# Splitting the last weight quarter four steps later, and issuing the conversion's first loads four steps earlier

## The chip, the cores and the metric

The kernel runs on one core of a Trainium2 chip. A core has five engines that work side by side, each with a queue of its own that it works off in order: PE (matmuls), DVE (vector work), ACT (activations and casts), POOL (GpSimd, here elementwise subtractions and indirect transfers) and SP, which issues most of the DMA transfers. They wait for each other on semaphores. The metric is the device time of one launch in microseconds (us).

## The reference, cut to what matters

Three networks follow each other on 3072 tokens of 320 numbers.

```python
x = attn(r, k, v, w, a, b)                   # a recurrence over 768 positions, 32 heads of 40
# mixture of 8 experts, one expert per token
h = relu(einsum('ecd,edf->ecf', disp, w1))   # 8 x (448 rows here) x 320 -> 1024
y = einsum('ecf,efd->ecd', h, w2)            # -> 320, times the gate's probability
# second network, all tokens; w_in and w_out are float64
h = x @ w_in                                 # 3072 x 320 -> 2048
g = where(h > 0, h, exp(min(h, 0)) - 1)
out = (g @ w_out).astype(float32)            # -> 3072 x 320
```

The change touches only the second and third of them (the experts and the second network).

## The kernel before, in words

The recurrence takes roughly the first 440 us and is not touched. After it, `ffn` runs 14 blocks: blocks 0 to 7 are the experts (448 token rows each, 8 steps), blocks 8 to 13 are the second network (512 rows each, 16 steps). A step (b, f) is one chunk of 128 hidden units of block b. `run` writes the program step by step, and every engine keeps that order. In a step the PE does `s1` (eight matmuls at line 968, which fill a `ph` bank), and then `s2` of an older step: three steps back within the experts, four within the second network. `s2` multiplies the activated chunk into the accumulators `po`. The activation of an expert's chunk is ACT's H (L1097) and DVE's L (L1098). In the second network it is DVE N, ACT E and M, DVE M and E, ACT H, and then L (L1112) on DVE for the first five steps of each sixteen, on POOL for the others.

Precision is kept by splitting every weight into a rounded part and a rest. `Weights.split` does this for a quarter of a weight set in four pieces: one ACT cast of 704 columns (L775) and four POOL subtractions (L780) a piece. The raw quarters lie in two buffers and the split ones in four (`ring`). The last of 20 quarters, number 19, is the fourth quarter of the second network, first read in step (8, 12). Its split goes into the buffer that the second half of expert 7 used, whose last reader is `s2` of step (7, 7). The lag puts that `s2` into step (8, 3). Directly behind it come the evictions of expert 7's accumulators (ACT L1044 and L1046, DVE L1045 and L1047), and these free the banks that the first `s2` of block 8 (L992 to L994) writes.

`extra(b, f)` is called at the end of each step and places the pieces. `more(b, f)` is called from it and moves the conversion on: `Convert.pieces` turns the float64 weights of the second network into float32 by integer work on DVE. Jobs 7 to 27 of 28 are left for this part, 21 of them: nine of 512 columns and twelve of 320. A job is three calls:

- stage 1: SP issues the load of the job after next (L822, L825), DVE does L858 and L859, SP issues the store of the job before (L830, L834);
- stage 2: DVE L864 and L865;
- stage 3: DVE L867, L869, L870.

A first call of its own, ahead of all jobs, issues the loads of the first two jobs. Odd steps make two calls and even steps one, from step (0, 5) on; stage 1 waits for its load. Loads go into three buffers S. SP's queue also carries the fetches of the raw quarters (L801, L803), one at every fourth step, and the tokens of the next block (L1084). A block's tokens are transposed by the PE (`pt`), cast by ACT (L952) and completed by DVE (XL and XS, L953) during the block before it.

Of the kernel before, what the change touches and what calls it, by code (L numbers as in the profile page):

```python
# [742 lines left out]
class Ring:  # L743
# [8 lines left out]
    def next(s, split):  # L752
        k = s.turn[split]
        s.turn[split] += 1
        return s.tile((1, 4, 6, 8)[k % 4], F32R) if split else s.tile((0, 3)[k % 2], F32)
# [39 lines left out]
def expert(nc, ring, w1, w2, e, paired=True):  # L795
    def load(g, R):
        q = R.rearrange("p (f x) -> p f x", x=704)
        c = slice(512 * g, 512 * g + 512)
        for k, (o, r, m) in enumerate(((0, 0, 128), (0, 128, 128), (0, 256, 64), (64, 256, 64))):
            k = min(k, 2)  # L800
            nc.sync.dma_start(out=q[o:o + m, :, 128 * k:128 * k + 128],  # L801
                              in_=w1[e, r:r + m, c].rearrange("p (f x) -> p f x", x=128))
        nc.sync.dma_start(out=q[:, :, 384:704], in_=w2[e, c, :].rearrange("(f p) d -> p f d", p=128))  # L803
    return Weights(nc, ring, load, 8, paired)
# [73 lines left out]
def ahead(W):  # L878

    W.fetch(0)  # L880
    yield
    yield from W.split(0)
    W.fetch(1)


def ffn(tc, nc, cst, disp, xt, w1, w2, w32, out, ring, W0, cv):
# [192 lines left out]
    def rows(src, gate=True):  # L1079

        def load(s, now):
            s.X = s.XF[:, 0:4 * RW].rearrange("p (i d) -> p i d", i=4)
            for i in range(4) if now else (slice(0, 4),):
                nc.sync.dma_start(out=s.X[0:112, i], in_=src[:, i])  # L1084
            yield
            if not gate:
                return
            yield
            g = yield from soft(s)
            for i in range(4):  # L1090
                nc.scalar.mul(s.X[0:112, i, 0:D], s.X[0:112, i, 0:D], g[:, i:i + 1])
            yield
        return load
# [61 lines left out]
    def run(blocks, extra):  # L1155

        n = len(blocks)
        lag, now = [], iter(())
        for b, B in enumerate(blocks):
            nf = B.W.nf  # L1160
            for f in range(nf):
                if f == 0 and b + 1 < n:
                    first, side = blocks[b + 1].load(), blocks[b + 1].prep()
                x = B.s1(f)
                lag.append((B, f, x))
                while len(lag) > B.back:
                    p = lag.pop(0)
                    p[0].s2(*p[1:])
                a, now = now, B.act(*x)
                next(now)  # L1170
                next(a, None)
                if b + 1 < n and next(first, 1) and f >= nf - 6:
                    next(side, None)
                extra(b, f)
        next(now, None)
        if isinstance(B, Turned):
            for p in lag:
                p[0].s2(*p[1:])
        else:
            B.finish([p[1:] for p in lag])  # L1180
# [8 lines left out]
    def experts(r, dyn=False, more=None):  # L1189
        Ws = [W0 if not dyn and e == 0 else expert(nc, ring, w1, w2, e, not dyn) for e in range(8)]  # L1190
        hs = [(W, h) for W in Ws for h in range(2)] + ([] if dyn else [(W2, g) for g in range(4)])

        bl = []
        for e in range(8):
            if dyn:
                src = dv[e, bass.ds(r, 1)].rearrange("r p i d -> (r p) i d")
                dst = yr[SL * e:SL * e + SL, :].rearrange("(i p) d -> p i d", p=112)

                def store(Y, i, dst=dst):
                    if i == 3:  # L1200
                        nc.sync.dma_start(out=dst, in_=Y[0:112])
                bl.append(Block(Ws[e], rows(src), relu, store, P=112))
            else:
                def store(Y, e=e):
                    c = bass.ds(over["base"][e - 1], SL) if e else slice(0, SL)
                    nc.sync.dma_start(out=xt[0:256, c].rearrange("(k p) n -> p k n", p=128), in_=Y[:, 0:2])
                    nc.sync.dma_start(out=xt[256:D, c], in_=Y[0:64, 2])
                    nc.sync.dma_start(out=xt[D:D + 1, c], in_=Y[64:65, 2])
                bl.append(Turned(Ws[e], rows(dv[e, 1], e > 0), relu, store, P=112))
        if dyn:  # L1210
            for _ in ahead(Ws[0]):
                pass
        n = len(hs)

        def fetch(j):
            if j < n:
                hs[j][0].fetch(hs[j][1])

        def split(j):
            if j < n:  # L1220
                yield from hs[j][0].split(hs[j][1])

        def go(x, k):
            for _ in range(k):
                next(x, None)
        go(split(1), 5)
        bl[0].start(0 if dyn else 26)
        fetch(2)
        gen = [iter(())]
        first = iter(()) if dyn else late_gate(bl[0])  # L1230
        next(first, None)

        def extra(b, f):
            if b >= 8:
                next(final, None)
                return
            if b == 0 and f > 1:
                next(first, None)
            i, ph = divmod(8 * b + f, 4)

            late = {(14, 0): 16, (14, 2): 17, (15, 2): 18}.get((i, ph)) if i > 13 else i + 2 if ph == 0 else None
            if late:
                gen[0] = split(late)
                fetch(late + 1)
            go(gen[0], 1 if i < 14 else 2)
            if more:
                more(b, f)
        final = split(19)
        if not dyn:
            bl += [sorted_block(g) for g in range(6)]  # L1250
        run(bl, extra)

    def late_gate(B):

        g = yield from soft(B, "late")
        yield
        p = ps.tile([128, 512], F32, tag="ph", name="pgate")
        for i in range(4):
            nc.tensor.matmul(p[:, 112 * i:112 * i + 112], g[:, i:i + 1].to_broadcast([112, 128]), ident[0:112, 0:112], start=True, stop=True)
        yield  # L1260
        B.G = ap.tile([128, SL], F32, tag="gate", name="gate", bufs=1)
        nc.scalar.copy(B.G, p[:, 0:SL])
# [3 lines left out]
    def sorted_block(g):  # L1266

        def load(s, now):
            s.X = s.XF.rearrange("p (k n) -> p k n", k=3)
            c = slice(512 * g, 512 * g + 512)  # L1270
            nc.sync.dma_start(out=s.X[:, 0:2], in_=xt[0:256, c].rearrange("(k p) n -> p k n", p=128))
            nc.sync.dma_start(out=s.X[0:64, 2], in_=xt[256:D, c])
            f = ap.tile([128, 4], F32, tag="idf", name="idf", bufs=3)
            with nc.allow_non_contiguous_dma("a token's number a row"):
                nc.sync.dma_start(out=f, in_=xt[D:D + 1, c].rearrange("o (i p) -> p (o i)", p=128))
            yield
            yield
            s.id = ap.tile([128, 4], I32, tag="id", name="id", bufs=3)
            nc.vector.tensor_copy(s.id, f)
            yield  # L1280
        def store(Y, i):
            x = nc.gpsimd.indirect_dma_start(  # L1282
                out=out, out_offset=bass.IndirectOffsetOnAxis(ap=B.id[:, i:i + 1], axis=0),
                in_=Y[:, i], in_offset=None, bounds_check=NTOK - 1, oob_is_err=False).ins
            for y in sent:
                tc.declare_no_dep(x, y, reason="scatters write different rows")
            sent.append(x)
            nc.gpsimd.memset(gap, 0.0)
        B = Sorted(W2, load, elu, store, back=4)
        return B  # L1290
# [116 lines left out]
    def more(b, f):  # L1407
        if b == 0 and 0 < f < 5 or b == 1 and f in (2, 7):
            next(ct, None)
        if b or f > 4:  # L1410
            for _ in range(1 + f % 2):
                next(rest, None)
    one = over["one"] = ap.tile([128, 8], F32, name="one", bufs=1)
    nc.gpsimd.memset(one, 1.0)
# [6 lines left out]
    nc.gpsimd.memset(cst["turn"], 0.0)  # L1421
    ct = counts()
    experts(0, more=more)
    for _ in rest:
        pass
# [62 lines left out]
```

## Time and profile before

| | us |
|---|---|
| median of 3 runs | 1066.04 (1063.58 to 1072.04) |
| profiled execution, its own time | 1064.33 |
| its span, first to last instruction | 1062.6 |
| PE busy | 965.8 (91% of the span) |
| DVE busy | 727.8 (68%) |
| POOL busy | 606.5 (57%) |
| ACT busy | 516.9 (49%) |

The mean granted clock of TensorE was 0.941 of full speed. The busy shares are means over stages that differ, so the table says which engine to look at first and not what holds it up. The profile's views used below are the list of waits (who waited for whom), the timeline (one engine's instructions in order, with the idle time before each in brackets and what ended it), the windows (busy time of each engine in a stretch, then PEclk, the share of the DMA engines and GB/s), the groups of instructions by form, and the chain that ended last.

### The profile page before, as it was taken

To read this page: it belongs to the slowest core of one execution; us is meant where nothing else is said; L and a number is where in the kernel's file an instruction comes from. 1 tells how busy PE (TensorE), PEld (TensorE's weight loads), DVE (VectorE), ACT (ScalarE), POOL (GpSimd) and SP (SyncE) were. 2 spreads that over 40 slices of the span, in tenths; PEclk is the share of its full clock that TensorE was granted. 3 is DMA by queue.
4 is the path that set the end of the run, shared out by engine and by line. 5 is a ranking of instruction groups with operands and counts; after the bars stand their busy time and mean duration, and the time that the engine had idled before them with its cause. 6 is when DMAs were issued, how large, how long until landed. Compare 5 with 4: busy or idle time off the path is not lost.

```text
span 1062.6 us, 25351 instructions
## 1 busy us (share of the span) xinstructions
PE 965.8 (91%) x9995; PEld 871.9 (82%) x9995; DVE 727.8 (68%) x1287; ACT 516.9 (49%) x1011; POOL 606.5 (57%) x926
## 2 busy tenths in 40 slices
PE   5869978899899999888999999989999999999993
PEld 4758877798788889677889888869989989989983
DVE  8856756788674677549798963656766767776751
ACT  4646544556463334244535545454555455554551
POOL 4757839899898813456677876733323333323332
PEclk9866988899899889999999999989999999999997
DMA  6768675667654864576877765400101010100000
GB/s 165 163 179 197 168 137 105 151 131 141 139 110 103 192 164 103 155 203 168 230 218 209 221 193 188 161 23 3 48 1 32 19 26 25 26 25 1 26 1 28
DMA packets 180984, 121.67 MB, mean 115 GB/s; under 512 B 105792, under 2 KB 166872, under 8 KB 179224
## 3 DMA queue, kind: packets, MB, share of 16 engines
q1 hardware_dynamic: 176788, 102.89, 39.6%
q0 software_dynamic: 3168, 11.14, 3.0%
q10 hardware_dynamic: 900, 5.93, 2.2%
q8 instruction: 81, 1.33, 0.6%
q14 instruction: 47, 0.39, 0.1%
HBM read 86.87 MB, written 33.05 MB: 113 GB/s over the span
## 4 chain that ended last, share of the span: by engine, by line
PE 28%; issue 10%; POOL 6%; DVE 6%; DMA 4%; ACT 2%; SPq 1%; POOLq 0%; DVEq 0%; ACTq 0%
PE ph L968 14%; PE po L992 4%; PE po L994 4%; PE po L993 4%; POOL ring L780 3%; POOL L L1112 2%; DMA ring<-in_w_dram 2%; DVE L L1098 1%; ACT ring L775 1%; SPq L801 1%; DMA S<-in_w_in_dram 1%; DMA w<-E 1%; POOL out_dram L1282 1%; DVE E L859 1%; DVE M L867 1%
## 5 line engine op out<-in xcount | busy, mean ns | idle before, releaser
L780 POOL TENSOR_TENSOR ring<-ring,ring 128x64 fp32r<-128x64 f32 (+2 forms) x320 | 195.7, 647 | 90.0 <-ACT ring L775 87.7
L1112 POOL TENSOR_TENSOR L<-E,H 128x512 fp32r<-128x512 f32 x66 | 87.6, 1327 | 185.8 <-ACT H L1111 148.2
L968 PE MATMUL ph<-XH,ring 128*128 128x512 f32 (+1 forms) x640 | 172.9, 392 | 4.4 <-DVE L L1098 3.9
L968 PEld LDWEIGHTS ph<-XH,ring 128*128 128x128 f32 x640 | 117.4, 193 | 19.6 <-DVE L L1098 4.5
L1105 ACT ACTIVATE E<-N 128x512 f32<-128x512 f32 x96 | 60.7, 633 | 143.7 <-DVE N L1104 88.0
L992 PE MATMUL po<-ring,H 128*128 128x320 f32 x384 | 119.6, 311 | 5.5 <-ACT Y L1044 5.3
L353 POOL TENSOR_TENSOR X<-X,ring 128x60 f32<-128x60 f32 (+19 forms) x170 | 114.9, 676 | 13.3
L994 PE MATMUL po<-ring,L 128*128 128x320 f32 x384 | 119.6, 311 | 1.5 <-POOL L L1112 1.5
L993 PE MATMUL po<-ring,H 128*128 128x320 f32 x384 | 119.4, 311 | 0.0
L1104 DVE TENSOR_SCALAR N<-ph 128x512 f32<-128x512 f32 x96 | 65.9, 686 | 47.4 <-PE ph L968 47.0
L968 PE MATMUL ph<-XL,ring 128*128 128x512 f32 (+1 forms) x320 | 97.6, 386 | 0.0
L968 PE MATMUL ph<-XS,ring 128*128 128x512 f32 (+1 forms) x320 | 97.5, 386 | 0.0
L351 POOL TENSOR_TENSOR ring<-X,ring 128x60 f32<-128x60 f32 (+19 forms) x108 | 74.2, 687 | 39.0 <-DMA ring<-dab 18.2
L992 PEld LDWEIGHTS po<-ring,H 128*128 128x128 f32 x384 | 72.6, 189 | 10.5 <-ACT Y L1044 5.7
L993 PEld LDWEIGHTS po<-ring,H 128*128 128x128 f32 x384 | 72.7, 189 | 4.1
L994 PEld LDWEIGHTS po<-ring,L 128*128 128x128 f32 x384 | 72.9, 190 | 2.0 <-POOL L L1112 2.0
L1109 DVE SCALAR_TENSOR_TENSOR M<-E,M 128x512 f32<-128x512 f32 x96 | 70.7, 736 | 5.5 <-ACT M L1106 5.5
L775 ACT CAST ring<-ring 128x704 fp32r<-128x704 f32 x80 | 61.4, 779 | 21.3 <-issue 8.2
L1110 DVE SCALAR_TENSOR_TENSOR E<-ph,M 128x512 f32<-128x512 f32 x96 | 66.4, 691 | 7.8
L968 PEld LDWEIGHTS ph<-XL,ring 128*128 128x128 f32 x320 | 61.1, 191 | 10.8
L968 PEld LDWEIGHTS ph<-XS,ring 128*128 128x128 f32 x320 | 60.8, 190 | 10.8
L1111 ACT CAST H<-E 128x512 fp32r<-128x512 f32 x96 | 59.2, 617 | 15.1 <-DVE E L1110 12.0
(238 smaller groups left out, 2164.2 us busy)
## 6 DMA issues: line engine op xcount, KB each, us to landing
ring<-in_w_dram SPq DMA_DIRECT2D x16, 640.0 KB
ring<-in_w_dram SPq DMA_DIRECT2D x32, 256.0 KB
RVU<-in_d_in_dram SPq DMA_DIRECT2D x48, 160.0 KB
dab<-AB SPq DMA_DIRECT2D x24, 256.0 KB
ring<-in_e_in_dram ACTq DMA_DIRECT2D x18, 321.6 KB
ring<-w SPq DMA_DIRECT2D x4, 1408.0 KB
disp<-ring SPq DMA_DIRECT2D x8, 575.8 KB
ring<-in_w_dram SPq DMA_DIRECT2D x32, 128.0 KB
```

Source lines behind the costliest of these rows:

```text
L351: nc.gpsimd.tensor_tensor(tv, X[:, 0:n, s:s + 1].to_broadcast([128, n, m]), N[:, s:s + 1, s + 1:e].to_broadcast([128, n, m]), op=ALU.mult)
L353: nc.gpsimd.tensor_tensor(X[:, 0:n, s + 1:e], X[:, 0:n, s + 1:e], tv, op=ALU.subtract)
L775: s.nc.scalar.copy(B[:, 0:704], r)
L780: s.nc.gpsimd.tensor_tensor(B[:, to], r[:, q], B[:, q].bitcast(F32), op=ALU.subtract)
L968: nc.tensor.matmul(p, l, r[:, 0:s.T], start=i == 0, stop=i == len(seq) - 1)
L992: nc.tensor.matmul(o, H[:, c], hb, start=f == 0, stop=False)
L993: nc.tensor.matmul(o, H[:, c], lb, start=False, stop=False)
L994: nc.tensor.matmul(o, L[:, c], hb, start=False, stop=f == s.W.nf - 1)
L1104: nc.vector.tensor_scalar(N, p, 0.0, None, op0=ALU.min)
L1109: nc.vector.scalar_tensor_tensor(out=M, in0=E, scalar=1.0, in1=M, op0=ALU.add, op1=ALU.mult)
L1110: nc.vector.scalar_tensor_tensor(out=E, in0=p, scalar=0.0, in1=M, op0=ALU.max, op1=ALU.add)
L1112: eng.tensor_tensor(L, E, H.bitcast(F32), op=ALU.subtract)
```

## The change

In block 8, quarter 19 is split in steps 4 to 7 and no longer in steps 0 to 3. In step (0, 1) the conversion makes its first call, which only issues loads. All later calls keep their steps, so each does the stage that followed before.

```diff
         def extra(b, f):
             if b >= 8:
-                next(final, None)
+                if b > 8 or f > 3:
+                    next(final, None)
                 return
...
     def more(b, f):
         if b == 0 and 0 < f < 5 or b == 1 and f in (2, 7):
             next(ct, None)
-        if b or f > 4:
-            for _ in range(1 + f % 2):
+        if b or f > 4 or f == 1:
+            for _ in range(1 if f == 1 and not b else 1 + f % 2):
                 next(rest, None)
```

The first place is ACT's queue at the start of block 8. Before:

```order
L1097 ACTIVATE H<-ph 128x448
L775 CAST ring_9053<-ring_8985 128x704
L1105 ACTIVATE E<-N 128x512
L1106 ACTIVATE M<-N 128x512
L1111 CAST H<-E 128x512
L775 CAST ring_9053<-ring_8985 128x704
L1105 ACTIVATE E<-N 128x512
L1106 ACTIVATE M<-N 128x512
L1111 CAST H<-E 128x512
L775 CAST ring_9053<-ring_8985 128x704
L1044 COPY Y<-po 128x448
L1046 COPY half<-po 64x448
```

And now, in the same place:

```order
L1097 ACTIVATE H<-ph 128x448
L1105 ACTIVATE E<-N 128x512
L1106 ACTIVATE M<-N 128x512
L1111 CAST H<-E 128x512
L1105 ACTIVATE E<-N 128x512
L1106 ACTIVATE M<-N 128x512
L1111 CAST H<-E 128x512
L1044 COPY Y<-po 128x448
L1046 COPY half<-po 64x448
```

The three casts of the split stood ahead of the eviction of expert 7; now all four stand behind it, and so do POOL's subtractions. PE's rows are the same in both.

The second place is SP's queue in expert 0, from the tokens of block 1 on (`ring` rows are fetches of raw quarters). Before:

```order
L1084 DMA X<-disp 112x4x329
L801 DMA ring_6517<-in_w_dram 128x4x128 x2
L801 DMA ring_6517<-in_w_dram 64x4x128 x2
L803 DMA ring_6517<-in_w_dram 128x4x320
L801 DMA ring_6667<-in_w_dram 128x4x128 x2
L801 DMA ring_6667<-in_w_dram 64x4x128 x2
L803 DMA ring_6667<-in_w_dram 128x4x320
L822 DMA S_6715<-in_w_in_dram 128x1024
L822 DMA S_6717<-in_w_in_dram 128x1024
L822 DMA S_6719<-in_w_in_dram 64x1024 x2
```

And now:

```order
L1084 DMA X<-disp 112x4x329
L801 DMA ring_6517<-in_w_dram 128x4x128 x2
L801 DMA ring_6517<-in_w_dram 64x4x128 x2
L803 DMA ring_6517<-in_w_dram 128x4x320
L822 DMA S_6554<-in_w_in_dram 128x1024
L822 DMA S_6556<-in_w_in_dram 128x1024
L801 DMA ring_6671<-in_w_dram 128x4x128 x2
L801 DMA ring_6671<-in_w_dram 64x4x128 x2
L803 DMA ring_6671<-in_w_dram 128x4x320
L822 DMA S_6719<-in_w_in_dram 64x1024 x2
```

Two loads of 512 KB each have moved ahead of one fetch of a raw quarter; the third load has kept its place behind it.

The third place is DVE's queue from the end of step (0, 5) on. Before:

```order
L953 TENSOR_TENSOR XL<-pt,XH 128x448
L858 TENSOR_SCALAR N<-S_6715 128x512
L859 SCALAR_TENSOR_TENSOR E<-S_6715,N 128x512
L1098 SCALAR_TENSOR_TENSOR L<-ph,H 128x448
L953 TENSOR_TENSOR XS<-pt,XS 64x448
L864 TENSOR_SCALAR N<-E 128x512
L865 SCALAR_TENSOR_TENSOR M<-S_6715,N 128x512
L1098 SCALAR_TENSOR_TENSOR L<-ph,H 128x448
L867 TENSOR_TENSOR M<-M,E 128x512
L869 TENSOR_SCALAR N<-S_6715 128x512
L870 SCALAR_TENSOR_TENSOR E<-N,M 128x512
L858 TENSOR_SCALAR N<-S_6717 128x512
```

And now:

```order
L953 TENSOR_TENSOR XL<-pt,XH 128x448
L858 TENSOR_SCALAR N<-S_6554 128x512
L859 SCALAR_TENSOR_TENSOR E<-S_6554,N 128x512
L864 TENSOR_SCALAR N<-E 128x512
L865 SCALAR_TENSOR_TENSOR M<-S_6554,N 128x512
L1098 SCALAR_TENSOR_TENSOR L<-ph,H 128x448
L953 TENSOR_TENSOR XS<-pt,XS 64x448
L867 TENSOR_TENSOR M<-M,E 128x512
L869 TENSOR_SCALAR N<-S_6554 128x512
L870 SCALAR_TENSOR_TENSOR E<-N,M 128x512
L1098 SCALAR_TENSOR_TENSOR L<-ph,H 128x448
L858 TENSOR_SCALAR N<-S_6556 128x512
```

An odd step did stage 3 of one job and stage 1 of the next, and an even step stage 2. Now an odd step does stages 1 and 2 of a job and the even step behind it stage 3.

## Rows read from the trace of the kernel before

**Rows 1.** Chain that ended last, second network: start, us, what.

```profile
712.02 1.86 PE ph L968 x8
...
943.99 1.87 PE ph L968 x8
```

**Rows 2.** Waits of PE, 446 to 712 us: total, times, longest.

```profile
PE po L992 <- ACT Y L1044: 5.3, 1, 5.3
PE ph L968 <- DVE L L1098: 3.9, 2, 3.4
...
PE po L1032 <- DVE Y L1045: 2.1, 2, 1.8
```

**Rows 3.** Timeline, PE and ACT, block 8: start, us, engine, [idle before <- releaser].

```profile
696.30 0.36 PE L1041 MATMUL po<-H,ring 128*128 128x448 f32 x1
696.75 0.78 ACT L775 CAST ring<-ring 128x704 fp32r<-128x704 f32 x1 [8.23 <-issue]
703.25 0.52 ACT L1044 COPY Y<-po 128x448 f32<-128x448 f32 x1
703.83 0.64 PE L992 MATMUL po<-ring,H 128*128 128x320 f32 x1 [5.30 <-ACT Y L1044]
...
710.10 0.31 PE L992 MATMUL po<-ring,H 128*128 128x320 f32 x1
```

**Rows 4.** Windows: busy PE, PEld, DVE, ACT, POOL; then PEclk, DMA share, GB/s.

```profile
703.00:706.00 3.00, 2.17 (x8) 2.17 (x9) 2.63 (x6) 1.64 (x4) 2.11 (x4) 0.50 0.33 123
```

**Rows 5.** Costliest groups of the page: busy, mean ns, idle before, releaser.

```profile
L1112 POOL TENSOR_TENSOR L<-E,H 128x512 fp32r<-128x512 f32 x66 | 87.6, 1327 | 185.8 <-ACT H L1111 148.2
```

**Rows 6.** Timeline, SP, DVE and PE, expert 0.

```profile
455.89 0.60 SPq L803 DMA_DIRECT2D ring<-in_w_dram  x1
...
468.92 2.54 SPq L822 DMA_DIRECT2D S<-in_w_in_dram  x4
...
477.44 0.43 DVE L858 TENSOR_SCALAR N<-S 128x512 int32<-128x512 int32 x1 [7.41 <-DMA S<-in_w_in_dram]
...
479.19 1.08 PE L968 MATMUL ph<-XH,ring 128*128 128x448 f32 x4 [3.44 <-DVE L L1098]
```

**Rows 7.** Timeline, PE, at three seams between experts.

```profile
493.46 0.44 PE L1031 MATMUL po<-H,ring 128*128 128x448 f32 x1 [2.61 <-DVE Y L1050]
...
500.24 0.74 PE L933 MATMUL pt<-ident,X 112*128 112x112 f32 x4
...
552.21 0.37 PE L1031 MATMUL po<-H,ring 128*128 128x448 f32 x1
...
560.71 0.55 PE L933 MATMUL pt<-ident,X 112*128 112x112 f32 x4
...
604.22 0.37 PE L1031 MATMUL po<-H,ring 128*128 128x448 f32 x1
...
609.11 0.97 PE L968 MATMUL ph<-XH,ring 128*128 128x448 f32 x4
```

**Rows 8.** Groups by form, DVE, 469 to 632 us: busy, mean ns.

```profile
L867 DVE TENSOR_TENSOR M<-M,E 128x512 f32<-128x512 f32 x9 | 8.3, 922 | 0.0
L869 DVE TENSOR_SCALAR N<-S 128x512 int32<-128x512 int32 x9 | 6.9, 768 | 0.0
L865 DVE SCALAR_TENSOR_TENSOR M<-S,N 128x512 f32<-128x512 uint32 x9 | 6.9, 766 | 0.3
L870 DVE SCALAR_TENSOR_TENSOR E<-N,M 128x512 f32<-128x512 int32 x9 | 6.9, 766 | 0.3
L864 DVE TENSOR_SCALAR N<-E 128x512 int32<-128x512 int32 x9 | 4.0, 448 | 0.1
```

**Rows 9.** Windows, columns as in Rows 4.

```profile
464.00:466.00 2.00, 1.55 (x10) 1.28 (x9) 1.55 (x3) 1.70 (x4) 1.97 (x4) 1.00 0.00 0
```

**Rows 10.** Timeline, POOL and DVE, expert 7.

```profile
663.73 12.57 POOL L780 TENSOR_TENSOR ring<-ring,ring 128x176 fp32r<-128x176 f32 x24
667.41 8.92 DVE L1279 CAST id<-idf 128x4 int32<-128x4 f32 x1
```

## The prediction

> **What bounds the kernel now.** I read the chain that ended last first, because only what lies on it can shorten the run. From 712.02 to 943.99 us it is the PE and nothing else: 65 rows of eight matmuls, 231.97 / 64 = 3.62 us apart [rows 1]. A step of the second network takes 3.62 us, and what the PE gains before block 8 moves the rest forward as it is. So the question is where the PE stood still before that. PE's own list of waits for 446 to 712 us answers it [rows 2]: one wait of 5.3 us for an ACT eviction, one of 3.4 us for DVE's L, two of 2.1 us together for a DVE eviction. A fourth, of 2.61 us, is in rows 7. The change touches the causes of all four.
>
> The timeline of block 8 shows the first [rows 3]. The last matmul that reads the old split buffer ends at 696.30 + 0.36 = 696.66. Only then, at 696.75, ACT starts the cast of quarter 19's first piece, after 8.23 us idle. Behind that cast, in ACT's queue, stand two more casts and the activations of steps (8, 1) and (8, 2), and behind these the eviction L1044, which starts at 703.25. The PE restarts at 703.83 after 5.30 us idle. Then it is slow: the window from 703 to 706 us has a granted clock of 0.50, the 1.2 GHz level [rows 4]. From 703.83 to 710.10 it needs 6.27 us for one step.
>
> The timeline of expert 0 shows the second [rows 6]. SP issues the first four S loads at 468.92, and DVE has stood idle 7.41 us, since 470.03, when it starts stage 1 at 477.44. L of the step stands behind it, and the PE loses 3.44 us.
>
> **The change part by part, and the sum.**
>
> *The split in steps 4 to 7.* The four casts leave their place ahead of the eviction, so L1044 can start when its bank is complete, before 696.66. From the start of L1044 to the PE's restart took 0.58 us [rows 3]. The PE has `s1` of its own until 698.53 (703.83 less 5.30), 1.87 us after 696.66, so I leave nothing of the wait. The slow step goes with it, since the PE ran without a pause up to there. Gain: 5.30 + (6.27 - 3.62) = 7.95 us. Ends: 5.3 if the clock falls all the same, 7.95 if not; I take the upper one.
>
> *The same work, later.* Four casts of 0.78 us [rows 3] and sixteen subtractions of 12.57 / 24 = 0.52 us [rows 10] come into steps 4 to 7. POOL's piece of 2.1 us and its own L of 1.33 us [rows 5] are 3.4 us of a step of 3.62 in steps 6 and 7; in 4 and 5 POOL has no L. What hides them is the lag of four steps, 14.5 us between L and the matmul that needs it. Without that cover, POOL's 2.1 us for each of two steps is 4.2 us. Quarter 19 is read in step 12 and is ready four steps earlier. Cost taken: 0.
>
> *The early loads.* SP issues two loads at 456.49 (455.89 + 0.60) [rows 6], some 0.6 us each (2.54 / 4). The next fetch in SP's queue belongs to a step three steps on, so it is not held. In the trace 1.5 MB landed from 468.92 to 477.44, behind a fetch, which is 5.7 us for these 1.0 MB. From 464 to 466 us the DMA engines moved nothing [rows 9], so the earlier fetch is over by 464, and the loads are there by 469.7 at the latest; stage 1 asks at 470.03. Gain: 3.44 us of the PE; at the other end, if they come with the fetch as now, 0.
>
> *The regrouped stages.* Stage 3 of a wide job costs 0.922 + 0.768 + 0.766 = 2.46 us, stage 2 costs 0.448 + 0.766 = 1.21 us [rows 8]. In the odd step ahead of each eviction DVE had stages 3 and 1; now it has 1 and 2, so 1.24 us less stands ahead of L1045 and L1050. Nothing is added: the 21 jobs do the same seven instructions each.
>
> *The seams between experts.* In a full-speed stretch the PE does `s2`, `s1`, `s2` in 609.11 - 604.22 = 4.89 us [rows 7]. At the first seam it waits 2.61 us and then needs 500.24 - 493.46 = 6.78 us for these, so 2.61 + 1.89 = 4.50 us are lost. At the third, 560.71 - 552.21 = 8.50 us hold the same work and the wait: 3.61 us lost. The rest of the DVE-eviction waits is 2.1 - 1.8 = 0.3 us [rows 2]. At the first seam DVE comes out 7.41 - 3.44 = 3.97 us earlier against the PE, and 1.24 for the regrouping, which is more than the 2.61 it was late: all 4.50 go. At the third only the 1.24 is sure against 1.8 late; I leave 0.55 and no slow step.
>
> Sum: 7.95 + 3.44 + 4.50 + 3.61 + 0.3 - 0.55 = 19.25 us. The profiled execution took 1064.33, so 1045.1. It lies 1.7 us below the median of the runs shown, so the median comes to 1046.8; I say **1047**.
>
> **A rule against it.** DVE's cast of 128x4 numbers took 8.92 us and ended at 676.33, while POOL ran 24 subtractions that ended at 676.30 [rows 10]. So one form of DVE instruction waits until POOL pauses. Stage 1 and stage 2 hold such single-input forms, and the change puts them back to back. Against a large cost: L869 and L864 are the same instruction on the same shape, and the dearer of them takes 0.768 us against 0.448 [rows 8], so the price of a neighbour on POOL was 0.3 us there and not a burst. The Trainium skill ("GPSIMD Engine Reference", section 1, Specifications) says that GpSimd shares its SBUF interfaces with VectorE, with contention for VectorE instructions in a two-port mode or with two SBUF inputs. By that rule the conversion could lose what the regrouping gives, and the sum would be the 11.4 us of the first rival below; the 8.92 us agree with it, the 0.768 us only faintly.
>
> **Rivals.**
> - *DVE stays late in the experts.* A wide job takes 2.46 + 1.21 us of it in two steps of 4.89 / 3 x 4 = 6.5 us, before stage 1, two L and the transposed tokens are counted, so removing one idle stretch may only shift the lateness to another seam. For it: the third seam was late with no load wait before it. Against: 1.24 us less ahead of every eviction. Then 7.95 + 3.44 = 11.4 remain: 1054.6. Late loads belong here too.
> - *The last seam's wait moves on.* The pieces in steps 4 to 7 hold POOL's L and DVE's catching up, and the PE stops once for 4.2 us and does one slow step of 2.65. For it: 3.4 of 3.62 us. Against: a lag of 14.5 us. Gain 19.25 - 6.85 = 12.4: 1053.6.
> - *Slower.* The back-to-back stages run into POOL's pieces as the 8.92 us cast did, and DVE becomes the bound of the experts. If each of 21 conversions loses 1 us on the path, half a piece, the time is 1066.0 - 7.95 + 21 = 1079. It decides at 7.95 / 21 = 0.38 us each, with the other gains of the experts gone. L869's 0.3 us speaks against it, and so does that POOL's bursts there are pieces and not 24 in a row.
> - *It does not do what it says.* The loads move but the eviction is still late because DVE's half of it (L1045) is: nothing but 3.4 us, 1062.6.
>
> **How the numbers follow.** Forecast 0.64; DVE stays late 0.16; wait moves on 0.10; no effect at the seams 0.04; slower 0.06. A measurement of this kernel can tell about 1% from no change, 10.7 us: faster is below 1055.4. The forecast and half of the first two rivals, which lie at that line, give 0.64 + 0.08 + 0.06 = 0.78; the rest of them and the case without effect give 0.16; slower 0.06. Below, the range ends where the 0.55 us go too and the median's offset is absent, with 2 us for its scatter: 1042. Above, it takes in both middle rivals, with 2 us for the same: 1057. That leaves out the last two, 0.10, and the tails of the others.
>
> **What would show it.** In the changed profile: ACT L1044 at block 8 starts within 1 us of its matmuls' end, and PE has no wait for it and PEclk stays at 1.00 there; DVE's L858 shows no idle for S in expert 0, and S is issued some 12 us earlier; no PE wait over 0.6 us for L1045 or L1050; L858, L864 and L869 keep their means within 0.2 us. I am wrong if DVE's busy time in the experts grows by more than a few us, if a PE wait for L (L1112) appears in steps (8, 8) to (8, 12), or if a seam between experts keeps a wait over 1 us with PEclk at half.

## The result, and the profile after

The changed kernel took 1049.88 us (median of 4 runs, 1043.23 to 1054.18) beside 1068.12 us for the kernel before. The ratio is 0.9844, 95% interval 0.9809 to 0.9878, so it is faster by some 16.7 us (13.0 to 20.4). Two later measurements of the same kernel gave 0.9883 (0.9806 to 0.9960) and 0.9874 (0.9840 to 0.9908), which is 12 to 13 us. All three gains are under 2%. The forecast was 1047 us, a ratio of 0.982 to the 1066.04 us known then. The range, 1042 to 1057, held. The gain came out smaller than the 19.25 us of the sum, by little in the first measurement and by more in the other two.

The profiled execution took 1050.7 us, its span is 1049.0. PE's list of waits from 446 to 712 us answers [rows 2]:

```profile
PE po L1037 <- DVE L L1098: 2.1, 1, 2.1
PE pt L933 <- DMA X<-disp: 1.9, 2, 1.1
PE po L1032 <- DVE Y L1045: 1.2, 1, 1.2
PE ph L968 <- ACT XH L952: 0.5, 1, 0.5
PE ph L968 <- DVE L L1098: 0.5, 1, 0.5
PE pt L933 <- ACT X L1091: 0.4, 1, 0.4
```

The 5.3, the 3.4 and the 2.6 us are gone. The two waits at the top of the new list were there before. What is left of the old causes is 1.2 us for L1045. One wait is new, 0.4 us for ACT L1091, the scaling of the next expert's tokens by their gate.

The timeline of block 8, ACT and PE, answers [rows 3]:

```profile
689.92 0.53 ACT L1044 COPY Y<-po 128x448 f32<-128x448 f32 x1 [0.35 <-PE po L1037]
690.14 0.37 PE L1041 MATMUL po<-H,ring 128*128 128x448 f32 x1
692.20 0.31 PE L992 MATMUL po<-ring,H 128*128 128x320 f32 x1
```

The eviction starts 0.22 us before the last matmul of its expert starts, since its own bank is complete, and L992 has no idle time before it. The window around it, columns as in [rows 4]:

```profile
689.00:692.00 3.00, 3.00 (x16) 2.52 (x15) 2.19 (x5) 1.63 (x3) 0.00 (x0) 1.00 0.02 8
```

The granted clock is 1.00, the 2.4 GHz level, where it was 0.50. In expert 0 (SP, then DVE; answers [rows 6]) the loads are issued at 459.58 and stage 1 starts with no idle time:

```profile
459.58 1.43 SPq L822 DMA_DIRECT2D S<-in_w_in_dram  x2
...
473.33 0.42 DVE L858 TENSOR_SCALAR N<-S 128x512 int32<-128x512 int32 x1
```

The seams between experts are where the gain fell short. PE and ACT at the first, PE and DVE at the third (answers [rows 7]):

```profile
495.35 0.36 PE L1039 MATMUL po<-L,ring 128*64 128x448 f32 x1
496.09 1.67 PE L933 MATMUL pt<-ident,X 112*128 112x112 f32 x4 [0.38 <-ACT X L1091]
497.53 1.06 PE L968 MATMUL ph<-XH,ring 128*128 128x448 f32 x4
...
495.47 1.92 ACT L1091 ACTIVATE X<-X,g 112x320 f32<-112x320 f32 x4 [1.37 <-DVE g L1076]
...
549.08 0.47 PE L1032 MATMUL po<-H,ring 128*128 128x448 f32 x1 [1.16 <-DVE Y L1045]
...
539.72 0.69 DVE L859 SCALAR_TENSOR_TENSOR E<-S,N 128x512 int32<-128x512 int32 x1 [1.87 <-DMA w<-E]
```

At the first seam four transposes run at the pace of ACT's L1091 and take 1.67 us, where they took 0.74 in the kernel before. (Other groups of four take 0.55 us where nothing holds them, and up to 1.63 at other seams.) At the third, L1045 is still late. The last row shows DVE 9.4 us earlier, standing 1.87 us for the store of an older job; from there to L1045, which starts at 548.41, DVE has no idle time. The cost of DVE's 512-wide forms, from 472 to 636 us, answers [rows 8]:

```profile
L859 DVE SCALAR_TENSOR_TENSOR E<-S,N 128x512 int32<-128x512 int32 x9 | 7.9, 874 | 3.1 <-DMA w<-E 2.8
L865 DVE SCALAR_TENSOR_TENSOR M<-S,N 128x512 f32<-128x512 uint32 x9 | 7.5, 837 | 0.3
...
L870 DVE SCALAR_TENSOR_TENSOR E<-N,M 128x512 f32<-128x512 int32 x9 | 6.9, 766 | 0.3
...
L867 DVE TENSOR_TENSOR M<-M,E 128x512 f32<-128x512 f32 x9 | 6.7, 740 | 0.1
...
L869 DVE TENSOR_SCALAR N<-S 128x512 int32<-128x512 int32 x9 | 5.6, 622 | 0.0
L864 DVE TENSOR_SCALAR N<-E 128x512 int32<-128x512 int32 x9 | 5.5, 610 | 0.3
L858 DVE TENSOR_SCALAR N<-S 128x512 int32<-128x512 int32 x9 | 4.8, 531 | 0.0
```

L864 became dearer (0.61 us against 0.45 before), L867 and L869 cheaper (0.74 against 0.92, 0.62 against 0.77): each of the three kept its work and changed its step, and its price changed with it.

To take a run apart I read the start of the first matmul of `s1` at a few steps, in every trace. A stretch between two such starts leaves out what moved both of them. The stretch from (0,5) to (1,1) holds the stage that waits for the loads, (1,1) to (6,1) the first five seams between experts, and (8,2) to (8,10) the wait in block 8. Each row is one trace:

| kernel | (0,0) starts | (0,5) to (1,1) | (1,1) to (6,1) | (6,1) to (8,2) | (8,2) to (8,10) |
|---|---|---|---|---|---|
| before | 449.66 | 17.67 | 148.89 | 58.04 | 36.85 |
| changed | 452.90 | 13.90 | 143.04 | 58.10 | 28.77 |
| changed, second trace | 450.84 | 13.91 | 144.17 | 59.68 | 28.77 |
| changed, third trace | 451.64 | 13.94 | 143.18 | 59.54 | 28.77 |
| split alone | 446.77 | 17.84 | 147.68 | 59.59 | 28.74 |
| conversion alone | 453.05 | 13.90 | 140.62 | 58.05 | 35.84 |
| early loads, old stages | 449.78 | 13.92 | 146.75 | 59.63 | 36.00 |
| new stages, late loads | 453.75 | 20.22 | 140.59 | 59.66 | 35.88 |
| no stage in step 1 | 449.28 | 13.94 | 142.23 | 59.56 | 28.74 |
| ten calls a block | 454.89 | 13.91 | 140.41 | 59.90 | 28.78 |
| ten calls, later cast | 445.65 | 13.95 | 141.45 | 55.73 | 28.77 |
| the same, step 2 free | 447.59 | 13.94 | 141.61 | 55.76 | 28.73 |
| POOL quiet | 447.18 | 13.90 | 140.71 | 56.11 | 28.77 |
| three buffers for E | 450.30 | 13.91 | 140.05 | 58.02 | 28.77 |

In the first two rows the parts are: start 3.24 us later; (0,0) to (1,1) 3.62 less (32.92 to 29.30); experts 5.85 less; (6,1) to (8,2) 0.06 more; block 8's stretch 8.08 less; the rest 0.65 more (336.24 to 336.89). The sum is 13.60, the difference of the spans. The split alone has the experts of the kernel before and took 147.68 us for them, so the 148.89 that the gains below are measured from is uncertain by some 1.2 us. The quoted expectations number these steps one too low: (0,4), (0,7), (1,3) there are (0,5), (1,0), (1,4), their "blocks 1 to 5" run from (1,1) to (6,1) and their "first eight steps of block 8" from (8,2) to (8,10).

### The profile page after: what moved, and what is told of

Same layout as the page of the kernel before. It is cut to its first block, busy times and chain, and to the rows that moved or that the text cites. A ratio compares the mean times of both kernels' runs of the same rounds, so it can differ in the third digit from the quotient of the medians.

```text
span 1049.0 us, 25349 instructions
## 1 busy us (share of the span) xinstructions
PE 963.1 (92%) x9995; PEld 868.3 (83%) x9995; DVE 726.2 (69%) x1287; ACT 514.5 (49%) x1011; POOL 614.4 (59%) x926
## 4 chain that ended last, share of the span: by engine, by line
PE 41%; DVE 7%; issue 3%; DMA 3%; ACT 2%; POOL 1%; SPq 0%; POOLq 0%; ACTq 0%; DVEq 0%
PE ph L968 21%; PE po L994 5%; PE po L993 5%; PE po L992 5%; DVE L L1098 1%; DMA w<-E 1%; ACT X L1091 1%; DVE E L859 1%; DVE N L864 1%; PE po L1037 1%; PE po L1039 1%; DMA xt<-Y 1%; DMA ring<-in_w_dram 1%; PE po L1038 1%; PE po L1033 1%
## 5 line engine op out<-in xcount | busy, mean ns | idle before, releaser
L1112 POOL TENSOR_TENSOR L<-E,H 128x512 fp32r<-128x512 f32 x66 | 94.3, 1429 | 166.6 <-ACT H L1111 154.4
L968 PE MATMUL ph<-XH,ring 128*128 128x512 f32 (+1 forms) x640 | 170.7, 388 | 0.9 <-ACT XH L952 0.5
L968 PEld LDWEIGHTS ph<-XH,ring 128*128 128x128 f32 x640 | 115.7, 189 | 15.3 <-ACT XH L952 0.9
L992 PE MATMUL po<-ring,H 128*128 128x320 f32 x384 | 118.5, 309 | 0.4 <-ACT H L1111 0.4
L992 PEld LDWEIGHTS po<-ring,H 128*128 128x128 f32 x384 | 72.1, 188 | 4.8 <-ACT H L1111 0.6
```

The source lines that it names most:

```text
L968: nc.tensor.matmul(p, l, r[:, 0:s.T], start=i == 0, stop=i == len(seq) - 1)
L992: nc.tensor.matmul(o, H[:, c], hb, start=f == 0, stop=False)
L1112: eng.tensor_tensor(L, E, H.bitcast(F32), op=ALU.subtract)
```

## The experiments

**The split alone.** Only the first part of the diff:

```diff
-                next(final, None)
+                if b > 8 or f > 3:
+                    next(final, None)
```

> Only the first part of the change: quarter 19 is split in steps 4 to 7 of block 8, the conversion stays as in the kernel before. Theory (the parts add up, and each gain stays where it was made): in the profile the wait of PE for ACT's eviction L1044 is gone, the first eight steps of block 8 take 28.8 us and not 36.85, the experts' seams stay as before (first seam's wait for L1050 about 2.6 us, step (0,7) late by 3.4 us). Gain 8.1 us on the chip, ratio about 0.992. Rival (the change of the conversion is needed for it, because DVE's half of the eviction is late too): the wait moves to L1045 and the gain is under 4 us, ratio above 0.996.

Median 1061.84 (10 runs) against 1068.42, ratio 0.9958 (0.9922 to 0.9994). The trace shows 28.74 us in block 8, 8.11 less, and the eviction (timeline, ACT) 0.20 us before the last matmul of its expert at 695.06:

```profile
694.86 0.53 ACT L1044 COPY Y<-po 128x448 f32<-128x448 f32 x1 [0.35 <-PE po L1037]
```

PE's waits, 446 to 712 us:

```profile
PE po L1032 <- DVE Y L1045: 2.0, 2, 1.8
PE po L1031 <- DVE Y L1050: 1.1, 1, 1.1
```

The third seam keeps its 1.8 us, and no wait appeared for L1045 in block 8. The first seam's wait for L1050 was 1.1 us and not the 2.6 expected, and the step behind the late loads waited 2.1 and not 3.4, with the same code in the experts. The trace puts the 8 us on the split alone. The runs show 4.5 us (0.6 to 8.3), so their interval just holds them.

**The conversion alone.** Only the second part:

```diff
-        if b or f > 4:
-            for _ in range(1 + f % 2):
+        if b or f > 4 or f == 1:
+            for _ in range(1 if f == 1 and not b else 1 + f % 2):
```

> Only the second part of the change: the conversion's first call at step (0,1), block 8 as in the kernel before. Theory: from the start of block 0 to the start of block 8 about 9.4 us less than before (239.85 us there, so about 230.4), of which block 0 some 3.6, block 1 some 2.9 and blocks 2 to 5 together 3.0; the 5.3 us wait for ACT L1044 stays. Ratio about 0.991. Rival (gains in the experts are taken back at the next wait): under 5 us to the start of block 8, ratio above 0.995.

Median 1059.26, ratio 0.9911 (0.9873 to 0.9949). From (0,5) to (1,1) 3.77 us less, in the experts 8.27 less; the 5.3 us for L1044 stay. In this trace ACT stood 3.28 us in block 0 until 459.32, for a raw quarter; the early loads were issued at 459.89, so it is not they that held it, but (0,0) to (1,1) gained only 1.29 us. The sum to block 8 is 9.5 us less (9.4 expected), so the theory holds in total, but its parts do not: block 0 gained 1.3 us where 3.6 was expected, block 1 gained 2.8 (2.9), and blocks 2 to 5 gained 5.4 where 3.0 was. That the sum fits is in part luck.

**Early loads with the old stages.**

```diff
-        if b or f > 4:
-            for _ in range(1 + f % 2):
+        if b or f > 4 or f == 1:
+            for _ in range(1 if not b and f in (1, 5) else 1 + f % 2):
```

> The early loads without the regrouping: the first call comes at step (0,1) and step (0,5) makes one call, so every stage keeps the step that it had in the kernel before. Block 8 as before. Theory A (two causes: the load made DVE late once, and stages 3 and 1 ahead of the eviction make each seam late): block 0 gains 3.6 us; block 1, where DVE is no longer behind from the load, gains part of its 4.5; the third seam stays late with a wait of about 1.8 us for L1045, as before. Gain to the start of block 8 5 to 7 us. Theory B (the late load was the only cause, DVE carried its lateness from seam to seam): the third seam's wait goes too, and the gain is that of the early loads with the regrouping, about 9.4 us. Theory C (the regrouping made the gain at the seams): only 3.6 us.

Ratio 0.9933 (0.9903 to 0.9962). The stretch of the load gained 3.75 us, the experts 2.14. All of the latter is at the first seam, 2.30 us (0.8 beside the trace of the split alone). The third seam stayed late (PE's waits, 446 to 712 us):

```profile
PE po L1032 <- DVE Y L1045: 1.7, 2, 1.5
...
PE po L1031 <- DVE Y L1050: 0.2, 1, 0.2
```

That is theory A, two causes. Its 5 to 7 us are all but met up to (6,1), 2.84 + 2.14 = 4.98 us; to (8,2) only 3.39 are left, as (6,1) to (8,2) took 1.59 more (see below).

**New stages with late loads.**

```diff
-            for _ in range(1 + f % 2):
+            for _ in range(3 if not b and f == 5 else 1 + f % 2):
```

> The regrouping without the early loads: step (0,5) makes three calls (the loads, then stages 1 and 2 of the first job), so the stages stand as in the change but the loads are issued where they were. Block 8 as before. Theory A: DVE again waits some 7 us for S, and PE stands 3.4 us or up to 1.2 us longer, since stage 2 now stands behind the wait too, ahead of L; the first seam keeps most of its wait for L1050 (1 to 2.6 us); the third seam is as in the change, 1.2 us of wait. Gain to the start of block 8 2 to 4 us. Theory B (DVE's lateness is carried on): no gain at any seam, the same time as before. Theory C (the regrouping made the gain at the seams): about 5.8 us.

Ratio 0.9956 (0.9916 to 0.9995). The stretch of the load takes 20.22 us from (0,5) to (1,1), 2.55 more than before. The wait itself hardly grew, 3.50 us beside 3.44. It is the step behind it, (1,0), that took 5.85 us at a granted clock of 0.53, where the kernel before took 3.39 at 1.00. Its first four matmuls (timeline, PE) took 1.86 us, and 1.08 before [rows 6]:

```profile
484.08 1.86 PE L968 MATMUL ph<-XH,ring 128*128 128x448 f32 x4 [3.50 <-DVE L L1098]
```

From (1,1) to (6,1) it is 140.59 us, 8.30 less, as little as with the conversion alone. PE has no wait for an eviction of experts 0 to 6 (the waits, 446 to 712 us):

```profile
PE ph L968 <- DVE L L1098: 5.4, 3, 3.5
PE po L992 <- ACT Y L1044: 5.3, 1, 5.3
PE po L1037 <- DVE L L1098: 2.1, 1, 2.1
PE pt L933 <- DMA X<-disp: 1.5, 2, 0.9
```

Theory A's total is met (3.42 us less to (8,2); 2 to 4 expected), but not its parts: the first seam was to keep 1 to 2.6 us and the third 1.2. The first seam does not tell who earned it, since the PE's slow step ahead of it left DVE 2.5 us more to catch up. (The split alone, with the old conversion, shows the same: step (1,0) took 4.90 us at a clock of 0.65, and the seam's wait was 1.1 us and not 2.6.) The seam has to be taken together with that step. The four kernels that have the two parts or not, by trace:

| kernel | (0,5) to (2,1) | (2,1) to (6,1) |
|---|---|---|
| before | 49.73 | 116.83 |
| early loads, old stages | 43.68 | 116.99 |
| new stages, late loads | 48.86 | 111.94 |
| conversion alone (both) | 43.13 | 111.38 |

Up to the end of the first seam's block the gain is the loads', 6.05 of 6.60 us; the regrouping alone gives 0.87, and none beside the 48.43 us of the split alone. Behind it the gain is the regrouping's, 4.89 of 5.45 us, and the loads alone give none. So C is right from the second seam on, and the loads earn their own stretch and the first seam.

**The changed kernel again, twice.**

> The changed kernel itself once more, as the measure of what varies by itself. Theory: what is before the change's first instruction varies from run to run, so the first matmul of block 0 starts anywhere from 446.8 to 453.8 us, as in the five traces so far; from the start of step (0,4) to the start of block 1 it takes 13.9 us, blocks 1 to 5 take 140.6 to 143.1 us together, block 8's first eight steps 28.8 us. Rival (the 3.2 us by which the changed kernel's trace starts block 0 later come from the change): the start stays within 0.5 us of 452.9 us.

Block 0 started at 450.84. Over all traces it starts from 445.65 to 454.89, with unchanged code ahead of it, so the 3.24 us later start is no effect of the change. What makes it vary is open. The third seam's wait was 1.24 us again and block 8 took 28.77. (1,1) to (6,1) took 144.17, over the 143.1 expected.

> The changed kernel, run beside the last version as its measure. Ratio to the kernel before between 0.981 and 0.989; first matmul of block 0 anywhere from 445.7 to 454.9 us; blocks 1 to 5 within 142.5 to 144.5 us; PE's wait for L after the cast of the tokens' numbers 2.0 to 2.4 us in block 7.

As expected: 0.9874 (0.9840 to 0.9908), (1,1) to (6,1) in 143.18 us, and 1.14 us of wait for L1045.

**No stage in the step ahead of the eviction.**

```diff
-        if b or f > 4 or f == 1:
-            for _ in range(1 if f == 1 and not b else 1 + f % 2):
+        for _ in range((1, 0, 1, 2, 2, 2, 2, 2)[f] if b or f > 4 else f == 1):
```

> The changed kernel with no stage of the conversion in step 1 of blocks 1 to 7: its two calls go to steps 4 and 6, which make two each, so a block has twelve calls as before. Theory P (what counts is what stands directly ahead of the eviction): the waits at steps 2 and 3 go, 1.65 us at the first seam and 2.19 us at the third, blocks 1 to 5 take about 138.5 us instead of 143.0, about 4 us less. Theory D (DVE has hardly an idle us in a block with twelve calls, so it is late wherever they stand): a wait for L or for the transposed tokens appears in steps 4 to 7, and blocks 1 to 5 take 142 us or more, no gain.

The waits at the seams went (the first seam's 3.56 + 5.25 us became 3.25 + 4.99), but waits for L in the later steps came. PE's list has 1.3 and 0.8 us for it; 0.9 of that is in step (0,5), where the changed kernel has 0.46 to 0.89 as well, and the rest, some 1.2 us, is new and lies in blocks 3 and 4. (1,1) to (6,1) took 142.23 us, 0.8 to 1.9 less than the changed kernel. That is theory D more than P: here a wait removed at one place came back at another. The ratio is 0.9854 (0.9776 to 0.9931).

**Ten calls a block.**

```diff
+        for _ in range((2, 0, 1, 1, 1, 1, 2, 2)[f] if b or f > 4 else f == 1):
```

> The changed kernel with ten calls a block instead of twelve (2, 0, 1, 1, 1, 1, 2, 2 in steps 0 to 7; block 0: 1, 2, 2 in steps 5 to 7), so none in the step ahead of the eviction and the conversion ends in block 6 instead of block 5. Both theories expect a gain: P because the step ahead of the eviction is empty, D because some 3 us a block of DVE's work are gone. Blocks 1 to 5 take 138 to 139 us instead of 143.0, block 6 27.6 to 28.5 us, the whole 3.5 to 5 us less than the changed kernel. Rival (the lateness at the first seam comes from the late transfers of tokens, or the conversion's end runs into the fetches of the last quarters in block 7): under 1.5 us.

(1,1) to (6,1) took 140.41 us, 2.6 to 3.8 less than the changed kernel; 138 to 139 was expected. The conversion alone, with twelve calls in the same places as the changed kernel, took 140.62, so this stretch does not show that ten calls are the better number. The first seam's step (1,4) kept its 5.31 us. The ratio, 0.9843 (0.9779 to 0.9906), does not tell it from the changed kernel.

**The cast of the tokens' numbers later.** On top of ten calls; the cast goes behind the loop of `Sorted.prep`, which puts it into step (7,6).

```diff
-            nc.vector.tensor_copy(s.id, f)
+            s.idf = f
...
+            nc.vector.tensor_copy(s.id, s.idf)
```

> As the kernel with ten calls a block, and the cast of the tokens' numbers (128x4, line 1279) moved from the step (7,2) to behind the last piece of the next block's tokens, step (7,5), where POOL's run of 24 subtractions is over. Theory: PE's wait of 2.1 us for DVE's L in block 7 goes, block 7 takes 28.2 us instead of 30.5, and nothing comes in its place: 2.3 us less than with ten calls alone, 1042 to 1044 us. Rival (the cast waits at its new place for the next run of subtractions, which starts in step (7,6)): the wait comes back there, for DVE's N or L, and block 7 stays at 30 us or more.

Ratio 0.9813 (0.9742 to 0.9885), median 1044.92. PE's 2.1 us for L are gone and (6,1) to (8,2) takes 55.73 us, 2.3 to 4.2 less than in the kernels with the early cast beside POOL's run. The wait went, but DVE's standstill did not. In the next kernel, timeline of DVE and POOL in block 7:

```profile
657.25 8.06 DVE L1062 TENSOR_TENSOR XL<-X,XH 128x512 fp32r<-128x512 f32 x1
665.23 0.61 DVE L1101 SCALAR_TENSOR_TENSOR L<-ph,H 128x448 fp32r<-128x448 f32 x1
665.77 0.68 DVE L1062 TENSOR_TENSOR XL<-X,XH 128x512 fp32r<-128x512 f32 x1
...
643.37 21.39 POOL L780 TENSOR_TENSOR ring<-ring,ring 128x64 fp32r<-128x64 f32 x40 [2.28 <-ACT ring L775]
```

Now the first XL takes 8.06 us instead of 0.68 and ends 0.55 us behind POOL's run (643.37 + 21.39 = 664.76). It stands one step behind the cast's old place, and the L behind it is needed one step later, so nobody waits.

**The same with step 2 free.** The pattern is (2, 0, 0, 2, 1, 1, 2, 2).

> As the kernel with ten calls a block and the later cast, with the call of step 2 moved to step 3 (2, 0, 0, 2, 1, 1, 2, 2), so that no stage stands between the two halves of the gate's softmax. Theory (the 1.4 us that the first seam still loses, a wait of the PE for ACT's L1091, comes from that stage): step (1,3) takes 3.9 to 4.3 us instead of 5.3, 1 us less in block 1 and nothing else moves; the whole 7 to 9 us less than the changed kernel run beside it, 1042 to 1045 us. Rival (two calls in step 3 make the tokens' XL in step 4 late): a wait for XL or L of 0.5 us or more appears in steps 4 to 7, blocks 1 to 5 take as long as with ten calls alone, 140.4 us or more.

Ratio 0.9825 (0.9796 to 0.9855), median 1046.4 beside 1051.84 for the changed kernel on the same chip, 5.4 us less where 7 to 9 was expected. The theory on the first seam fell: its step still took 5.30 us. The second half of the softmax is behind an L that waits for H (timeline, DVE):

```profile
489.45 0.62 DVE L1101 SCALAR_TENSOR_TENSOR L<-ph,H 128x448 fp32r<-128x448 f32 x1 [1.41 <-ACT H L1100]
```

**POOL quiet beside the conversion.** ACT copies in place of POOL's subtractions, so the weights of experts 1 to 7 are not split.

```diff
             s.nc.scalar.copy(B[:, 0:704], r)
+            if s.quiet:
+                s.nc.scalar.copy(B[:, 704:1408], r)
+                yield
+                continue
...
+        for W in Ws[1:]:
+            W.quiet = not dyn
```

> The changed kernel, with the rests of the weights of experts 1 to 7 not subtracted by POOL: ACT copies 704 columns in place of each piece's four subtractions (so these weights are no longer split, which the time does not depend on). POOL stands still beside the conversion in blocks 1 to 5. Theory (DVE is late at the seams because its conversion is dearer beside POOL's pieces): DVE's 512-wide forms take 0.42 us for L858, L864, L869 (0.53, 0.61, 0.62 us in the changed kernel) and 0.69 us for L859, L865, L867, L870 (0.87, 0.84, 0.74, 0.77 us), PE's waits for L1045 and L1091 in blocks 1 and 3 go, blocks 1 to 5 take 138 to 139.5 us instead of 143.0. Rival (the place of the stages alone makes the lateness): the means fall but the third seam keeps more than 1 us of wait, blocks 1 to 5 take over 141.5 us.

DVE's 512-wide forms, with L numbers six higher (L864 is the changed kernel's L858), from 472 to 636 us:

```profile
L876 DVE SCALAR_TENSOR_TENSOR E<-N,M 128x512 f32<-128x512 int32 x9 | 6.2, 693 | 0.3
L873 DVE TENSOR_TENSOR M<-M,E 128x512 f32<-128x512 f32 x9 | 6.2, 687 | 0.1
...
L865 DVE SCALAR_TENSOR_TENSOR E<-S,N 128x512 int32<-128x512 int32 x8 | 5.5, 693 | 2.6 <-DMA w<-E 2.4
L871 DVE SCALAR_TENSOR_TENSOR M<-S,N 128x512 f32<-128x512 uint32 x8 | 5.5, 693 | 0.3
...
L875 DVE TENSOR_SCALAR N<-S 128x512 int32<-128x512 int32 x9 | 3.8, 421 | 0.0
...
L870 DVE TENSOR_SCALAR N<-E 128x512 int32<-128x512 int32 x8 | 3.4, 427 | 0.3
L864 DVE TENSOR_SCALAR N<-S 128x512 int32<-128x512 int32 x8 | 3.3, 413 | 0.0
```

The means are those expected, and the waits for L1045 and L1091 are no longer in PE's list. The first seam's four transposes still took 1.68 us at L1091's pace, so that part did not go with POOL's pieces. The one run took 1043.56 us. The time of the stretch did not follow: 140.71 us and not 138 to 139.5. ACT has twice the copies there, which may be why; this was not separated. So the experiment settles the price of the neighbour, not what it costs the run.

**Three buffers for E.** The tag E, shared by the conversion and the second network, gets a third buffer.

```diff
-        return [ap.tile([128, 512], I32, tag=x, name=x) for x in "NEM"]
+        return [ap.tile([128, 512], I32, tag=x, name=x, bufs=3 if x == "E" else 2) for x in "NEM"]
...
-        N, E, M = (ap.tile([128, 512], F32, tag=x, name=x) for x in "NEM")
+        N, E, M = (ap.tile([128, 512], F32, tag=x, name=x, bufs=3 if x == "E" else 2) for x in "NEM")
```

> The changed kernel with three buffers for the tile E in place of two, so that stage 1 of a job no longer waits for the store of the job two before it (DVE's L859 stood 6.1 us in all for these stores in experts 1 to 5, once 1.87 us in step (2,7), some 7 us ahead of the third seam's eviction). Theory S (this wait is what makes DVE late at the third seam): L859's waits for stores go to under 1 us in all, the third seam's wait for L1045, 1.14 to 1.24 us in three traces, goes to under 0.3 us, block 3 takes 27.7 to 28.2 us instead of 29.8 and blocks 1 to 5 140.5 to 141.5 us instead of 143.0 to 144.2. Rival (it is the price of the stages beside POOL's pieces and their place ahead of the eviction; the store's wait is slack that DVE would spend waiting for H anyway): the wait for L1045 stays over 0.8 us, blocks 1 to 5 within 142.5 to 144.2 us. Either way the first seam keeps its 1.3 us for L1091 and block 7 its 2.1 us.

The trace is as theory S said. L859 no longer appears in DVE's list of waits from 470 to 640 us, where the changed kernel has

```profile
DVE E L859 <- DMA w<-E: 6.1, 7, 1.9
```

At the third seam PE runs through (timeline):

```profile
545.17 0.37 PE L1031 MATMUL po<-H,ring 128*128 128x448 f32 x1
545.37 0.36 PE L1032 MATMUL po<-H,ring 128*128 128x448 f32 x1
```

(1,1) to (6,1) takes 140.05 us, the least of all, and the third seam's block 27.74 instead of 29.78. Median 1043.98 (4 runs), ratio 0.9826 (0.9756 to 0.9897). By the medians it and the kernel with ten calls and the later cast (1044.92) lie under the changed kernel (1049.88, 1052.43, 1051.84), but the intervals of the ratios overlap. Three buffers and the later cast together were not tried. One thing speaks against settling on this: the two kernels with the new stages and the old split also had no wait at the third seam, with two buffers, and took 140.62 and 140.59 us for the stretch. There the same L859 stood 0.93 and 1.03 us for the store; in the three traces of the changed kernel it stood 1.87, 2.38 and 1.47. This fits a wait that makes the seam late only where it is long; why it was shorter in those two is open, and a third buffer is not shown to gain more than 0.6 us beside them.

## Why the prediction was right, and where its sum was off

The mechanism was right in all three places: PE's waits of 5.3, 3.4 and 2.6 us went with the causes named for them. The sizes of the first two were right, that of the seams was not.

- *The split, 7.95 us:* right, 8.08 to 8.11 by the traces of the kernel before and of those without the wait. Both halves are there, the 5.30 and the slow step. Where the wait stayed, the stretch took 35.84 to 36.85 us, so the slow step was worth 1.8 to 2.8 us and the split 7.1 to 8.1. The four pieces in steps 4 to 7 cost nothing: from 700 us to the end PE waited twice for L1112, 1.5 us in all, and that is what it waited for it in the second network before.
- *The early loads, 3.44 us:* right, 3.77.
- *The seams, 4.50 + 3.61 + 0.3 - 0.55 = 7.86 us:* this is the term that was mis-sized; 5.85 came, 4.7 and 5.7 in the other two traces. At the third seam 0.55 us were to be left; the block gained 1.07 us instead of 3.06, and 1.14 to 1.24 us of wait for L1045 stayed, against the sign of at most 0.6. The term assumed that DVE is late only by what the conversion puts ahead of L1045. It left out the wait for a store, 1.47 to 2.38 us ahead of this seam, and with a third buffer for E both waits went. At the first seam all 4.50 were to go, and 1.65 stayed. Some 1.3 of it is a wait of 0.38 us and the transposes' 1.67 us at the pace of ACT's L1091; behind the eviction's wait they had taken 0.74. So 3.92 of the 7.56 us at these two seams came. Gains at the second and fifth seam (1.44 and 1.29) were not in the sum, nor a loss of 0.79 at the fourth; that they bring the total up to 5.85 is luck. The shortfall is not in every trace: the conversion alone runs the same instructions in the experts in the same order and gained 8.27 us, 2.98 of them at the third seam. What made the changed kernel's three traces 2.4 to 3.6 us slower there is open beyond that store.
- *The cause given for the first seam* was right: DVE coming out 3.97 us earlier by the loads, with 1.24 by the regrouping on top. Together with its stretch the loads alone gain 6.05 us up to (2,1), the regrouping alone 0.87. For the seams behind it the prediction named the regrouping, and there the regrouping gains 4.89 and the loads nothing.
- *The rest between 19.25 and what was measured* is not tied to the change by any run: the start of block 0 varies by 9 us between traces, (0,0) to (0,5) takes 15.3 to 17.7 us, and (6,1) to (8,2) takes 58.0 to 59.9 us in kernels with the early cast beside POOL's run. Where it takes the longer time, the stretch behind PE's 2.1 us wait has a lower granted clock: 0.76 in the second trace of the changed kernel from 670 to 677 us, and 1.00 in the first.
- *The rule against the change* had its price in reach but not its direction. Beside POOL the seven forms of a wide job take 4.98 us in the changed kernel and 5.15 before, against 4.03 with POOL quiet (sums of the means). So nearly 1 us per job was paid before and after; putting the stages back to back added none, and DVE's busy time from (0,0) to (8,2) did not grow. The means of the wide forms kept within 0.2 us, as said. The Trainium skill ("GPSIMD Engine Reference", section 1, Specifications) names VectorE instructions with two SBUF inputs, or in a two-port mode, as those that contend. The quiet kernel agrees for the first kind, 0.74 to 0.87 us beside POOL against 0.69, and an instruction with one SBUF input and one from PSUM (L1098) keeps its 0.62 us in both. The forms with one input are dearer beside POOL too, 0.53 to 0.62 us against 0.41 to 0.43, and the cast that the prediction took as agreeing has one input; whether these run in a two-port mode no run shows.
- *A slip in the chances:* half of 0.10 is 0.05 and not 0.06, so the chance of faster comes to 0.77 and that of no clear change to 0.17. It changes nothing.

## What to carry to other kernels

When one wait is removed, list what else ends within the next microseconds at the same place: at two seams the gain ended at something that the sum had left out (a store's buffer, a neighbour's scaling). A stage's place is best tested by moving the place and the transfer separately. When the results are read, a stretch has to hold the stall together with what it delays: the first seam alone seemed to credit the regrouping, because the PE had lost the time one step earlier. Run the same code more than once before a stretch of 1 or 2 us is explained; here the same experts took from 140.6 to 144.2 us.

## What the hardware showed that was not expected

A 128x512 subtraction with two SBUF inputs took 8.06 us and ended where POOL's run of 40 subtractions did, as the 128x4 cast did in its place (8.95 us in the changed kernel, 0.16 us in the quiet one at the same step). In the experts, L867, also with two SBUF inputs, cost 0.74 us on average beside POOL. Why one kind of run holds DVE to its end and the other only slows it is open.
